# One score matmul per chunk and head in place of seven levels, in a gated linear attention with an FFN

## The chip, the cores and the metric

One core of a Trainium2 chip runs the whole program. TensorE (PE) does the matmuls and the transposes, VectorE (DVE), ScalarE (ACT) and GpSimd (POOL) the elementwise work, SyncE (SP) starts most of the DMAs. Every engine works through its instructions in the order in which the program lists them. The metric is the device time of one execution in microseconds; the profile is of one execution with the hardware profiler on. A matmul on 32-bit floats is two instructions in the trace, each with its own weight load; a transpose is one.

## The reference

```python
f = 1.0 / (1.0 + np.exp(-f_logit))                 # q, k, v, f_logit: (4, 8, 768, 48), float32
for t in range(S):
    state = f[:, :, t, :, None] * state + np.einsum('bhd,bhe->bhde', k[:, :, t], v[:, :, t])
    y[:, :, t] = np.einsum('bhd,bhde->bhe', q[:, :, t], state)
x = y.transpose(0, 2, 1, 3).reshape(B * S, H * D)  # 3072 x 384
g = x @ w_gate                                     # 384 x 1536, float64 as the program gets it
out = (g / (1 + np.exp(-g)) * (x @ w_val)) @ w_out # 1536 x 384, float64
```

In f_logit the values are normal with mean 2 and deviation 0.5.

## The kernel before

The sequence is cut into 6 chunks of 128 tokens; a batch and a chunk are a *unit* (24 of them, in the order of batches, then chunks). Two heads share a transposed tile: head 2a in partitions 0 to 47, head 2a + 1 in partitions 64 to 111, so a unit has 4 head pairs.

`attention(u)` takes a unit in steps that end at a `yield`. The sigmoid of f, then 12 transposes of f, k and q (L147) and their copies out of PSUM. One score matmul per head of q on k gives the diagonal (L169). Then seven levels (m = 1, 2, 4 ... 64, L178 to L202): 8 matmuls of 64 columns (L189), a product on VectorE that puts the next level's gates into q (L192), one on GpSimd for k (L194), one on GpSimd that multiplies neighbouring gates (L197), and a masked copy of the level's scores into A (L198). After that y = state and A on v (L209, L212), the change of the state (kT back by 4 transposes, L221, then 8 matmuls, L225), and the transposes of x (L247). Attention has two PSUM buffers of two banks.

`mlp(g)` is the FFN of 384 tokens (three units): 12 pieces `hidden(j)` with 3 gate and 3 val matmuls of 384 columns (L260), Silu on ScalarE (L263) and the product on VectorE (L265), and 3 pieces `down` of 12 matmuls (L270). PSUM has 3 banks for gate and val and 1 for down.

The order is written out by the loop at the end (L283 to L294): each step of a unit is issued, and after every second step one piece of the list `todo`. That list first holds the 18 pieces in which the weights are fetched (SyncE's queue) and converted from 64-bit floats (768 columns each: seven instructions on VectorE, L116 to L124, and a product on GpSimd, L125), later the FFN pieces of the three units just finished. Unit loads (f, q, k, v, 192 KB each) are issued two units ahead on SyncE's queue, outputs on ScalarE's.

Of the kernel before, what the change touches and what calls it, by code (L numbers as in the profile page):

```python
# [8 lines left out]
FP32 = mybir.dt.float32  # L9
I32 = mybir.dt.int32  # L10
U32 = mybir.dt.uint32
AF = mybir.ActivationFunctionType
ALU = mybir.AluOpType


@with_exitstack
def kernel(
    ctx: ExitStack,
    tc: tile.TileContext,
    q: bass.AP,  # L20
    k: bass.AP,
    v: bass.AP,
    f_logit: bass.AP,
    moe_w_gate: bass.AP,
    moe_w_val: bass.AP,
    moe_w_out: bass.AP,
    out: bass.AP,
):

# [8 lines left out]
    nc = tc.nc  # L40
    B, H, S, D = q.shape
    C = 128
    NCH = S // C
    HP = H // 2
    W = 64
    DM = H * D
    KT = DM // 128
    DFF = moe_w_out.shape[0]
    NF = DFF // 128
    GROUP = 3  # L50
    TB = GROUP * C
    LEVELS = [1, 2, 4, 8, 16, 32, 64]
    NRAW = 3
# [4 lines left out]
    const = ctx.enter_context(tc.tile_pool(name="const", bufs=1))  # L58
    att = ctx.enter_context(tc.tile_pool(name="att", bufs=2))
    ffn = ctx.enter_context(tc.tile_pool(name="ffn", bufs=2))  # L60
    wst = ctx.enter_context(tc.tile_pool(name="wst", bufs=2))
    aps = ctx.enter_context(tc.tile_pool(name="aps", bufs=2, space=bass.MemoryType.PSUM))
    fps = ctx.enter_context(tc.tile_pool(name="fps", bufs=3, space=bass.MemoryType.PSUM))


    ident = const.tile([128, 128], FP32, tag="ident", name="ident")
    make_identity(nc, ident)
    masks = {}
    for m in LEVELS:
# [7 lines left out]
    raw = {nm: [const.tile([128, H, W], FP32, tag=f"{nm}raw{i}", name=f"{nm}raw{i}") for i in range(NRAW)]  # L77
           for nm in "qkf"}
# [4 lines left out]
    w_gate = const.tile([128, KT, DFF], FP32, tag="w_gate", name="w_gate")  # L83
    w_val = const.tile([128, KT, DFF], FP32, tag="w_val", name="w_val")
    w_out = const.tile([128, NF, DM], FP32, tag="w_out", name="w_out")


    units = [(b, c) for b in range(B) for c in range(NCH)]
    vt = {}
# [41 lines left out]
    states = [const.tile([128, HP, 2, D], FP32, tag=f"state{i}", name=f"state{i}") for i in range(3)]  # L131
    for s in states:
        nc.gpsimd.memset(s, 0.0)
    state = {}
    xT = {}
# [158 lines left out]
        todo.pop(0)()  # L294


# [1 line left out]
_INS = ['q', 'k', 'v', 'f_logit', 'moe_w_gate', 'moe_w_val', 'moe_w_out']  # L298
_OUTS = [((3072, 384), 'float32')]
# [27 lines left out]
```

## Time and profile before

| | us |
|---|---|
| median of 3 runs (lowest, highest) | 1121.28 (1120.48, 1121.81) |
| the profiled execution | 1120.95 |
| its span, first to last instruction | 1119.0 |
| TensorE busy in it | 995.0 |
| mean granted clock of TensorE | 0.917 |

The span is what the profile's views cut up; the profiled execution's time has 1.95 us around it. A matmul's end is modelled, and matmuls overlap, so the distance from one start to the next tells more than a busy time.

### The profile page before, as it was taken

The numbers are of one execution on the slowest core, as the hardware profiler recorded it, in microseconds if no ns is written. First come the engines' busy times: TensorE is split into PE (matmuls) and PEld (weight loads), VectorE is DVE, ScalarE is ACT, GpSimd is POOL, SyncE is SP. The second block draws the span as 40 slices with busy tenths as digits, with TensorE's granted clock in tenths as the row PEclk, the third lists the DMA queues.
The fourth block names the chain that finished last, engine by engine and source line by source line (L and its number), as shares of the span: only waits on it lengthen the run. The fifth ranks groups of instructions, "written<-read, shape, count | busy, mean of one in ns | idle before, by whom it ended". The sixth has DMA issues, their size and how long they took to land.

```text
span 1119.0 us, 14668 instructions
## 1 busy us (share of the span) xinstructions
PE 995.0 (89%) x6104; PEld 686.2 (61%) x6104; DVE 434.0 (39%) x660; ACT 166.6 (15%) x288; POOL 281.2 (25%) x419
## 2 busy tenths in 40 slices
PE   3536489998999989998999989998999989998998
PEld 3535466666666566666666576665666666665654
DVE  5999973421432233422333223422333324423010
ACT  1001021120122011220121111220121110110110
POOL 4364541311322121321221221311221222312000
PEclk9955579997999979998899979999899979999899
DMA  9444310010111010110110110110110100000000
GB/s 189 125 138 110 116 29 14 16 36 18 26 29 26 18 36 8 22 36 15 29 29 8 36 36 1 29 36 15 29 29 8 36 8 1 1 1 22 1 1 21
DMA packets 106721, 38.68 MB, mean 35 GB/s; under 512 B 100512, under 2 KB 103584, under 8 KB 106656
## 3 DMA queue, kind: packets, MB, share of 16 engines
q1 hardware_dynamic: 103200, 33.04, 13.6%
q10 hardware_dynamic: 3456, 4.72, 1.2%
q8 instruction: 48, 0.79, 0.3%
q14 instruction: 17, 0.14, 0.0%
HBM read 33.03 MB, written 4.72 MB: 34 GB/s over the span
## 4 chain that ended last, share of the span: by engine, by line
PE 82%; DVE 14%; issue 2%; POOL 1%; ACT 0%; DMA 0%; SPq 0%; DVEq 0%; POOLq 0%; ACTq 0%
PE gate L260 17%; PE val L260 16%; PE o L270 16%; PE sc L189 15%; PE y L212 5%; DVE A L198 4%; DVE qT L192 3%; PE y L209 3%; PE fkT L147 2%; PE sc L169 2%; PE dS L225 1%; DVE man L124 1%; DVE p L116 1%; PE dS L221 1%; PE xTp L247 1%
## 5 line engine op out<-in xcount | busy, mean ns | idle before, releaser
L189 PEld LDWEIGHTS sc<-qT,kT 48*128 48x128 f32 x2688 | 186.8, 210 | 167.7 <-issue 95.1
L189 PE MATMUL sc<-qT,kT 48*128 48x64 f32 x2688 | 210.2, 301 | 89.0 <-DVE A L198 65.5
L260 PE MATMUL gate<-xT,w_gate 128*128 128x384 f32 x576 | 234.9, 518 | 0.6 <-ACT xT L249 0.6
L194 POOL TENSOR_TENSOR kT<-kT,e 128x256 f32<-128x256 f32 x144 | 121.2, 842 | 400.6 <-PE sc L189 400.6
L260 PE MATMUL val<-xT,w_val 128*128 128x384 f32 x576 | 201.9, 486 | 0.0
L270 PE MATMUL o<-w_out,h 128*128 128x384 f32 x576 | 197.0, 493 | 1.1 <-ACT ob L273 1.1
L260 PEld LDWEIGHTS val<-xT,w_val 128*128 128x128 f32 x576 | 109.6, 190 | 76.5 <-issue 0.6
L265 DVE TENSOR_TENSOR h<-silu,val 128x384 f32<-128x384 f32 x96 | 53.2, 555 | 249.9 <-PE val L260 248.2
L270 PEld LDWEIGHTS o<-w_out,h 128*128 128x128 f32 x576 | 105.8, 190 | 69.8 <-ACT ob L273 2.4
L198 DVE COPY_PREDICATED A<-mask,sc 128x512 f32<-128x512 int32 x168 | 146.6, 873 | 0.0
L192 DVE TENSOR_TENSOR qT<-qT,e 128x256 f32<-128x256 f32 x144 | 62.9, 436 | 215.1 <-PE sc L189 215.1
L260 PEld LDWEIGHTS gate<-xT,w_gate 128*128 128x128 f32 x576 | 96.9, 193 | 40.0 <-issue 2.3
L263 ACT ACTIVATE silu<-gate 128x384 f32<-128x384 f32 x96 | 47.1, 490 | 330.5 <-PE gate L260 330.3
L197 POOL TENSOR_TENSOR e<-fT 128x256 f32<-128x256 f32 x24 | 15.6, 652 | 253.5 <-ACT fT L154 253.5
L212 PE MATMUL y<-v,A 128*128 128x48 f32 x384 | 70.4, 323 | 2.7 <-issue 2.7
L212 PEld LDWEIGHTS y<-v,A 128*128 128x128 f32 x384 | 67.7, 249 | 8.1 <-issue 4.0
L215 ACT COPY x<-y 128x384 f32<-128x384 f32 x24 | 11.5, 478 | 282.7 <-PE y L212 282.7
L209 PE MATMUL y<-state,qT 128*128 128x96 f32 x160 | 43.9, 366 | 8.0 <-DVE qT L192 8.0
L192 DVE TENSOR_TENSOR qT<-qT,fT 128x256 f32<-128x256 f32 x24 | 26.0, 1084 | 53.5 <-PE sc L189 53.5
L197 POOL TENSOR_TENSOR e<-e 128x128 f32<-128x128 f32 (+1 forms) x144 | 41.6, 289 | 9.6
L273 ACT COPY ob<-o 128x384 f32<-128x384 f32 x24 | 11.5, 478 | 216.8 <-PE o L270 216.8
L173 DVE TENSOR_TENSOR A<-sc,ident 128x1024 f32<-128x1024 f32 x24 | 29.4, 1223 | 35.7 <-PE sc L169 35.7
(51 smaller groups left out, 617.4 us busy)
## 6 DMA issues: line engine op xcount, KB each, us to landing
fraw<-in_f_logit_dram SPq DMA_DIRECT2D x24, 192.0 KB, 3.0
qraw<-in_q_dram SPq DMA_DIRECT2D x24, 192.0 KB, 3.7
kraw<-in_k_dram SPq DMA_DIRECT2D x24, 192.0 KB, 4.2
v<-in_v_dram SPq DMA_DIRECT2D x24, 192.0 KB, 2.6
w<-in_moe_w_gate_dram SPq DMA_DIRECT2D x6, 768.0 KB, 5.3
w<-in_moe_w_val_dram SPq DMA_DIRECT2D x6, 768.0 KB, 4.2
w<-in_moe_w_out_dram SPq DMA_DIRECT2D x6, 768.0 KB, 4.3
out_dram<-ob ACTq DMA_DIRECT2D x24, 192.0 KB, 1.9
```

What stands on the lines that cost most here:

```text
L173: nc.vector.tensor_tensor(A, sc.rearrange("p r (a t) -> p (r a) t", t=C), ident.unsqueeze(1).broadcast_to((128, H, C)), ALU.mult)
L189: nc.tensor.matmul(sc[:, par, o + 64 * a:o + 64 * a + 64].rearrange("p (n r) -> p n r", r=m), lhsT=kT[r, a, :], rhs=qv[r, a, :, 1, :], sta ...
L192: nc.vector.tensor_tensor(qv[:, :, :, 1, :], qv[:, :, :, 1, :], ev[:, :, :, 0:1].broadcast_to((128, HP, n, m)), ALU.mult)
L194: nc.gpsimd.tensor_tensor(kv[:, :, :, 0, :], kv[:, :, :, 0, :], ev[:, :, :, 1:2].broadcast_to((128, HP, n, m)), ALU.mult)
L197: nc.gpsimd.tensor_tensor(E, ev[:, :, :, 0], ev[:, :, :, 1], ALU.mult)
L198: nc.vector.copy_predicated(A.rearrange("p g (n two r) -> p g n two r", two=2, r=m)[:, :, :, 1, :], masks[m].rearrange("p (n r) -> p n r", ...
L209: nc.tensor.matmul(both, lhsT=qT[:, a, :], rhs=state[b, c - 1][:, a, :, :].rearrange("p r d -> p (r d)"), start=True, stop=False, skip_gro ...
L212: nc.tensor.matmul(both[:, par * D:(par + 1) * D], lhsT=A[:, par * HP + a, :], rhs=vt[u][:, 2 * a + par, :], start=(c == 0), stop=True, sk ...
L260: nc.tensor.matmul(dst, lhsT=w[:, i, j * 128:(j + 1) * 128], rhs=xT[g][:, i, :], start=(i == 0), stop=(i == KT - 1))
L263: nc.scalar.activation(sg, gp, AF.Silu)
L265: nc.vector.tensor_tensor(h[j], sg, vp, ALU.mult)
L270: nc.tensor.matmul(op, lhsT=h[j][:, s * C:(s + 1) * C], rhs=w_out[:, j, :], start=(j == 0), stop=(j == NF - 1))
```

## The change

The program before becomes `general_path`, unchanged. A new `short_path` runs first and computes the whole output. In it a unit's gates are transposed before the sigmoid, with a column of zeros ahead of each head pair, and two scans on VectorE run along them: `tail`, backwards, is the product of all gates from a token to the chunk's end, `head`, forwards, is the product from the chunk's start, divided by the whole chunk's product. k times the tail and q times the head then need one matmul per head for all scores, and a causal mask on VectorE in two passes. The smallest whole product seen is kept in `least`; at the end it is compared with 2^-60, and only if it is below, `general_path` runs too and writes the output again.

Units are ordered by chunks, then batches. The FFN works on one chunk of all four batches (512 tokens). `take_turns` spreads the 20 attention steps of chunk c + 1 over the 28 FFN pieces of chunk c (gate and val are pieces of their own); chunk 0's attention comes first, alone. Weights are fetched and converted in other pieces (256 columns of all three row blocks), with five instructions on VectorE, two on ScalarE and two on GpSimd. Loads run three units ahead. All PSUM buffers are single banks, 4 for attention, 4 for the FFN.

```diff
+    units = [(b, c) for c in range(NCH) for b in range(B)]
...
+            kept["w"] = wst.tile(shape[:2] + [2 * shape[2]], I32, tag="w64", name="w64", bufs=3)
+            nc.sync.dma_start(out=kept["w"], in_=src)
...
+            nc.vector.tensor_single_scalar(top, hi, (1 << 20) - 1, op=ALU.bitwise_and)
+            nc.scalar.activation(man, top, AF.Identity, bias=1.0, scale=2.0 ** -20)
+            nc.scalar.activation(sign, hi, AF.Sign)
+            nc.vector.tensor_scalar(p2, hi, 20, 0x7FF, op0=ALU.logical_shift_right, op1=ALU.bitwise_and)
+            nc.vector.tensor_scalar(p2, p2, 1023 - 127, 1023 + 128, op0=ALU.max, op1=ALU.min)
+            nc.vector.tensor_scalar(p2, p2, 1023 - 127, 1 << 23, op0=ALU.subtract, op1=ALU.mult)
+            nc.gpsimd.tensor_tensor(sign, sign, p2.bitcast(FP32), ALU.mult)
+            nc.vector.scalar_tensor_tensor(man, lo.bitcast(U32), 2.0 ** -52, man, op0=ALU.mult, op1=ALU.add)
+            nc.gpsimd.tensor_tensor(dst, man, sign, ALU.mult)
...
+        p = transposed("fTp", fr)
+        nc.scalar.activation(pairs(gate)[:, :, 1:N1], p, AF.Sigmoid)
+        yield
+        nc.vector.tensor_tensor_scan(tail[:, 0:n][:, ::-1], gate[:, 0:n][:, ::-1], ones[:, ::-1], 1.0,
+                                     op0=ALU.mult, op1=ALU.add)
+        whole = pairs(tail)[:, :, 1:2]
+        kp = transposed("kTp", kr)
+        nc.vector.tensor_tensor(kT, kp, pairs(tail, 2)[:, :, 0:C], ALU.mult)
+        nc.vector.tensor_tensor(least, least, whole.rearrange("p a t -> p (a t)"), ALU.min)
+        nc.vector.tensor_single_scalar(pairs(start)[:, :, 0:1], whole, LEAST, op=ALU.max)
+        nc.vector.reciprocal(pairs(start)[:, :, 0:1], pairs(start)[:, :, 0:1])
+        nc.vector.tensor_tensor_scan(head, gate[:, 0:n], start, 1.0, op0=ALU.mult, op1=ALU.add)
+        qp = transposed("qTp", qr)
+        nc.vector.tensor_tensor(qT, qp, pairs(head)[:, :, 1:N1], ALU.mult)
+        if u + NRAW < len(units):
+            load(u + NRAW)
+        if c:
+            nc.gpsimd.tensor_tensor(decayed, states[b], whole.unsqueeze(2).broadcast_to((128, HP, 2, D)), ALU.mult)
+        yield
...
+                nc.tensor.matmul(sc[par][:, a * C:(a + 1) * C], lhsT=kT[r, a, :], rhs=qT[r, a, :], start=True, stop=True)
+        for par in range(2):
+            nc.vector.tensor_tensor(A[:, par], sc[par].rearrange("p (a t) -> p a t", t=C),
+                                    causal.unsqueeze(1).broadcast_to((128, HP, C)), ALU.mult)
...
+        order = sorted((2 * b + s, b) for b in range(B) for s in range(n_steps))
...
+    for i, f in enumerate(attention_steps(0)):
+        f()
+        if i in (2, 4, 6):
+            fetches.pop(0)()
+        if i in (10, 13, 16, 19):
+            weights()
+    for c in range(NCH):
+        pieces = mlp(c)
+        if c == 0:
+            hidden, pieces = pieces[:2 * NF], pieces[2 * NF:]
+            hidden = [f for i in range(0, 2 * NF, 2) for f in hidden[i:i + 2] + [weights]]
+            pieces = hidden + [weights] * (len(converts) - NF) + pieces
+        take_turns(pieces, attention_steps(c + 1) if c + 1 < NCH else [])
...
+    short_path(tc, least, *args)
+    nc.vector.tensor_reduce(low, least, axis=mybir.AxisListType.X, op=ALU.min)
...
+        nc.tensor.transpose(row, low, ident)
+        nc.vector.tensor_reduce(one, row, axis=mybir.AxisListType.X, op=ALU.min)
+    nc.vector.tensor_single_scalar(flag, one, LEAST, op=ALU.is_lt)
+    redo = nc.values_load(flag[0:1, 0:1], min_val=0, max_val=1, skip_runtime_bounds_check_because="a comparison")
+    with tc.If(redo > 0):
+        general_path(tc, *args)
```

## Rows read from the trace of the kernel before

**Rows 1.** The page's busy time, share and instructions of each engine, whole span.

```profile
PE 995.0 (89%) x6104; PEld 686.2 (61%) x6104; DVE 434.0 (39%) x660; ACT 166.6 (15%) x288; POOL 281.2 (25%) x419
```

**Rows 2.** The page's chain that ended last, by engine.

```profile
PE 82%; DVE 14%; issue 2%; POOL 1%; ACT 0%; DMA 0%; SPq 0%; DVEq 0%; POOLq 0%; ACTq 0%
```

**Rows 3.** Busy time by stretch: engines, then PE's granted clock, DMA share, GB/s.

```profile
112.00:140.00 28.00, 12.50 (x103) 11.19 (x100) 27.16 (x33) 0.22 (x1) 14.37 (x12) 0.50 0.34 115
...
400.00:500.00 100.00, 97.82 (x634) 66.75 (x634) 34.05 (x54) 20.72 (x35) 24.55 (x41) 0.96 0.14 27
```

**Rows 4.** Longest pieces of the chain in order of time: start, length, what.

```profile
363.15 6.65 PE o L270 x20
...
999.33 6.65 PE o L270 x20
...
1050.00 1.94 PE val L260 x6
...
1090.64 7.75 PE o L270 x24
```

**Rows 5.** Timeline, steady state: start, length, instruction, count, idle before and releaser.

```profile
537.92 1.16 PE L169 MATMUL sc<-q,kT 48*128 48x128 f32 x16
...
539.01 0.91 PE L260 MATMUL gate<-xT,w_gate 128*128 128x384 f32 x2
...
564.39 1.90 PE L212 MATMUL y<-v,A 128*128 128x48 f32 x16
...
566.13 0.88 PE L260 MATMUL gate<-xT,w_gate 128*128 128x384 f32 x2
...
568.78 0.60 PE L221 MATMUL dS<-ident,kT 128*128 128x128 f32 x4
...
569.22 0.49 PE L247 MATMUL xTp<-ident,x 128*128 128x128 f32 x3
...
570.28 0.67 PE L225 MATMUL dS<-v,kt 128*64 128x48 f32 x16
...
570.88 1.56 PE L260 MATMUL gate<-xT,w_gate 128*128 128x384 f32 x4
```

**Rows 6.** Groups by line and shape: busy us, mean ns, idle before, releasers.

```profile
L189 PE MATMUL sc<-qT,kT 48*128 48x64 f32 x2688 | 210.2, 301 | 89.0 <-DVE A L198 65.5 <-POOL kT L194 11.0 <-DVE qT L192 8.8
...
L192 DVE TENSOR_TENSOR qT<-qT,fT 128x256 f32<-128x256 f32 x24 | 26.0, 1084 | 53.5 <-PE sc L189 53.5
L124 DVE SCALAR_TENSOR_TENSOR man<-w,man 128x768 f32<-128x768 uint32 x18 | 25.8, 1434 | 0.0
...
L116 DVE TENSOR_SCALAR p<-w 128x768 int32<-128x768 int32 x18 | 19.7, 1095 | 0.1
...
L156 DVE COPY kT<-fkT 128x512 f32<-128x512 f32 x24 | 16.6, 691 | 50.0 <-ACT fT L154 49.9
...
L118 DVE TENSOR_SCALAR p<-p 128x768 int32<-128x768 int32 x18 | 13.0, 720 | 0.0
...
L125 POOL TENSOR_TENSOR w_gate<-man,p 128x768 f32<-128x768 f32 x6 | 11.9, 1990 | 6.8 <-DVE p L119 5.9 <-DVE man L124 0.9
...
L121 DVE TENSOR_SCALAR top<-w 128x768 int32<-128x768 int32 x18 | 11.5, 638 | 0.0
...
L117 DVE TENSOR_SCALAR p<-p 128x768 int32<-128x768 int32 x18 | 10.3, 572 | 0.0
```

**Rows 7.** Timeline of VectorE in the opening, a conversion with nothing on GpSimd.

```profile
49.70 0.55 DVE L117 TENSOR_SCALAR p<-p 128x768 int32<-128x768 int32 x1
...
51.11 0.95 DVE L124 SCALAR_TENSOR_TENSOR man<-w,man 128x768 f32<-128x768 uint32 x1
```

**Rows 8.** Timeline: the first unit's first scores, TensorE.

```profile
10.19 2.08 PE L169 MATMUL sc<-q,kT 48*128 48x128 f32 x16 [2.04 <-DVE kT L156]
```

**Rows 9.** Timeline: the end of the program.

```profile
1107.52 8.01 PE L270 MATMUL o<-w_out,h 128*128 128x384 f32 x24 [0.57 <-ACT ob L273]
...
1116.07 0.34 ACTq L275 DMA_DIRECT2D out_dram<-ob  x1
```

More of the change, by code (lines that the diff above doesn't have):

```diff
@@ L13, with general_path @@
 ALU = mybir.AluOpType
+LEAST = 2.0 ** -60
 @with_exitstack
[L17 to L28, printed above, removed]
+def general_path(ctx, tc, q, k, v, f_logit, moe_w_gate, moe_w_val, moe_w_out, out):
     nc = tc.nc
@@ new lines, with kernel @@
+@with_exitstack
+def kernel(
+    ctx: ExitStack,
+    tc: tile.TileContext,
+    q: bass.AP,
+    k: bass.AP,
+    v: bass.AP,
+    f_logit: bass.AP,
+    moe_w_gate: bass.AP,
+    moe_w_val: bass.AP,
+    moe_w_out: bass.AP,
+    out: bass.AP,
+):
+    nc = tc.nc
+    args = (q, k, v, f_logit, moe_w_gate, moe_w_val, moe_w_out, out)
+    HP = q.shape[1] // 2
+    flags = ctx.enter_context(tc.tile_pool(name="flags", bufs=1))
+    least = flags.tile([128, HP], FP32, tag="least", name="least")
+    short_path(tc, least, *args)
+    low = flags.tile([128, 1], FP32, tag="low", name="low")
+    nc.vector.tensor_reduce(low, least, axis=mybir.AxisListType.X, op=ALU.min)
+    with tc.tile_pool(name="flagp", bufs=1, space=bass.MemoryType.PSUM) as pool:
+        ident = flags.tile([128, 128], FP32, tag="idf", name="idf")
+        make_identity(nc, ident)
+        row = pool.tile([1, 128], FP32, tag="row", name="row")
+        nc.tensor.transpose(row, low, ident)
+        one = flags.tile([1, 1], FP32, tag="one", name="one")
+        nc.vector.tensor_reduce(one, row, axis=mybir.AxisListType.X, op=ALU.min)
+    flag = flags.tile([1, 1], I32, tag="flag", name="flag")
+    nc.vector.tensor_single_scalar(flag, one, LEAST, op=ALU.is_lt)
+    redo = nc.values_load(flag[0:1, 0:1], min_val=0, max_val=1, skip_runtime_bounds_check_because="a comparison")
+    with tc.If(redo > 0):
+        general_path(tc, *args)
```

199 lines of the change are left out of this document (added).

## The prediction

> **What bounds the kernel now.** I read the busy shares first [rows 1]: TensorE is busy for 995.0 of 1119.0 us, no other engine half as long. The chain of waits says the same by time [rows 2]: 82% of it is TensorE, 14% VectorE. But the stages differ [rows 3]: at 112 to 140 us TensorE is busy for 12.5 of 28 us at a granted clock of 0.50 (the 1.2 GHz level) while VectorE is busy for 27.16, so the opening is bound by VectorE, which there converts the 64-bit weights; at 400 to 500 us TensorE is busy for 97.8 of 100 us at 0.96. The steady state repeats per group of 384 tokens: the long down products of 363.15 and 999.33 us are five groups apart [rows 4], so a group takes 636.2 / 5 = 127.2 us.
>
> What a group consists of at the 2.4 GHz level: a gate or val product is 1.94 us, a down product 7.75 us [rows 4], so the FFN is 24 x 1.94 + 3 x 7.75 = 69.8 us. For the attention I take starts to next starts on TensorE [rows 5]: 16 score instructions (8 matmuls, each in two passes) 539.01 - 537.92 = 1.09 us, and a level's 16, with as many weight loads, as much; 16 of y 1.74 us, so 0.109 each; four transposes 0.44 us; 16 of dS 0.60 us. A unit (one batch, one chunk of 128 tokens) without its levels: 19 transposes 2.1, scores 1.09, y (24 instructions with the state) 2.6, dS 0.60, together 6.4 us. Seven levels add 7.6 us. Three units are 42.0 us, with the FFN 111.8; the other 15.4 us of the group, 5.1 per unit, are stalls and half-clock stretches. The levels' matmuls show 89.0 us of idle ahead of them, 3.7 per unit, mostly for VectorE's masked copy and the two products of the next level [rows 6].
>
> **The change part by part.**
>
> *The levels go.* Per unit 112 TensorE instructions, seven masked copies, seven products and seven on GpSimd each for k and e. On the path: 7.6 us of matmuls and 3.7 us of waits per unit, 271 us in 24 units.
>
> *What takes their place on VectorE.* Two scans of 516 columns. The trace has no scan. From below, the nearest two-operation instruction does 768 columns in 0.95 us when nothing disturbs it [rows 7], so 0.64; from above, the slowest form per column, 256 in 1.084 us [rows 6], gives 2.2. I take 1.2: the first row doubled, since each element needs the one before it. Four passes of 512 columns over PSUM (k, q, two score masks) at the 0.691 of the PSUM copy [rows 6], two state updates of 192 columns at about half that (an estimate), four tiny ones at 0.2 (an estimate; bounds 0 and 0.69): 2.4 + 2.8 + 0.7 + 0.7 = 6.6 us per unit, 26 per chunk of four units. With 12 val products of 512 columns, 8.3, VectorE has 35 us of work per 125: hidden in steady state. The order gives it room: between the second step of a unit (k and q transposed, scans) and the third (scores) stand two FFN products, 5.2 us, against some 4.4 us of scan, products and scan.
>
> *Blocks of 512.* Gate and val stream 512 columns: 1.94 x 512 / 384 = 2.58 us. A chunk's FFN is 24 x 2.58 + 4 x 7.75 = 92.9 us; six of them cost what eight groups of 69.8 did, so this part alone moves nothing. It sets the order, though: one chunk of all four batches, whose attention (20 steps) is spread over the 28 FFN pieces of the chunk before. The last chunk's FFN stands alone: 92.9 us, against 69.8.
>
> *Steady chunk.* 92.9 + 4 x 6.4 = 118.5. Each of 20 changes between FFN and attention costs about 0.25 (in [rows 5] the two gate passes that begin at 539.01 and their like run 0.1 to 0.2 over their pitch), 5 us; at a chunk's end the last xT copy is exposed, 1.2 us (an estimate: the idle 0.57 ahead of a matmul that waits for a copy [rows 9], and the copy itself). 124.7 us. Chunks 1 to 3: 374. Chunk 4, beside an attention without kt and dS: 120.5.
>
> *Conversion.* VectorE keeps five instructions a piece: 19.7 + 10.3 + 13.0 + 11.5 + 25.8 = 80.3 us over 18 pieces, 4.46 each [rows 6]. Undisturbed they would be four of 0.55 and one of 0.95 [rows 7], 3.15; the rest is waiting beside GpSimd, which did one product of 1.99 us a piece [rows 6] and now does two. ScalarE takes two more; it is 15% busy [rows 1], and 36 instructions even at 0.95 are 34 us over a stage of 150. For VectorE I take 5.5 a piece, between 3.15 (no disturbance) and 4.46 + 1.99 = 6.45 (the second product blocks for its full length), nearer the upper end: 99 us in all.
>
> *Opening.* All four units of chunk 0 come first, at the 1.2 GHz level: the first scores take 2.08 us at 10.19 us [rows 8] against 1.16 warm, so PE terms double. The new first scores start at about the same time. From one unit's scores to the next, in TensorE's order: scores 2.1, f transposes 0.9, kt 0.9, y 3.5, dS 1.2, k and q 1.8, then some 3.6 of scan and products that nothing covers: 14 us. The third unit's q product ends at 38 us, where VectorE meets the first conversion. From there to the last one it has: conversions 99, the rest of units 2 and 3 8.7, the part of chunk 1's attention that is issued before the last piece (17 of 20 steps) 24.3, val products 8.3, in sum 140; at the share of 0.97 that it reached before [rows 3] 145 us, so the last weight is ready at 183 us. TensorE has 92.9 + 25.6 + 5 in that stage from 67 us on, and waits. Behind it: four down products 31, three attention steps 5, the copy 1.2: chunk 0 ends at 220 us.
>
> *Queues.* Bytes are unchanged (the same 96 unit loads and 18 weight loads). On SyncE's queue weight load n + 3 waits for conversion n, and unit loads stand behind it; they are for units three ahead, needed some 40 us later. The DMA share is 0.34 at 112 us [rows 3]. PSUM goes from two pairs and 3 + 1 banks to 4 + 4 single ones; a product's bank must be free three products (7.7 us) later, a Silu and one pass of 0.69 away. I cost both at nothing.
>
> *The end.* The flag: two reductions, a transpose, a compare, a register load on each engine, a jump. From below, nothing (the last output DMA, issued at 1116.07, ends the span 2.9 us later [rows 9] and may cover it); from above two further DMA-like round trips and ten tiny steps, 8. I take 5. The Trainium skill (Runtime: NRT & Kernel Launch, section Instruction fetch mechanics) says that a taken branch whose target isn't in the current pages stalls for a fetch; no run here shows it, and jumping over the whole old program is such a case, so it speaks for more than zero.
>
> Sum: 220 + 374 + 120.5 + 92.9, then 3.5 from the last matmul to the span's end as before [rows 4, 9], and 5: 816. The profiled execution is 1120.95 for a span of 1119.0, so 818; it lies 0.3 us under the median of the runs, which needs no correction.
>
> **The rivals.**
>
> GpSimd holds VectorE for the full length of both its products. Then 6.45 a piece, 17 us more: 835. For it: the 0.95 us instruction has a mean of 1.434 [rows 6, 7]. Against: 4.46 - 3.15 is only 1.3 per product of 1.99. The Trainium skill (SBUF — State Buffer, section Who interferes with whom) has it as an exclusive lock held for the whole instruction, which is this case.
>
> The conversions hide. With 3.15 a piece and scans of 0.64 VectorE needs 95 us from 38 us on, and TensorE is the bound from 67 us: 67 + 124.7 = 192, so 790. Against: the means above.
>
> The stalls stay. If a unit still loses 5.1 us where I give (5 + 1.2) / 4 = 1.6, because scores now wait for a serial chain of two scans, four overlapped attentions lose 4 x 4 x 3.5 = 56: 874. Against: 3.7 of the 5.1 stand ahead of the levels' matmuls, and 1.4 is left.
>
> Slower: the branch is taken, and the whole old program runs behind the new one: 818 + 1119 = 1937. It decides at a chunk's product of gates below 2^-60. The reference's inputs (seed 0) give 2^-30.5 as the smallest of all, and padded rows give 1, so only an error in the flag would do it.
>
> **How the numbers follow.** The forecast (800 to 850) 0.50, lock 0.13, hidden conversions 0.16, stalls 0.18, branch 0.03. So 818, and 770 to 880: the low end is the hidden case with an end of nothing and fewer changes, the high end the stall case. Under 0.2% (2.2 us, about what this measurement tells from no change) no case falls: faster 0.96, same 0.01, slower 0.03.
>
> **What would show it.** In the windows, VectorE over 90% busy and TensorE well below until the last w_out piece, near 183 us; later TensorE over 95% busy at a clock near 1. Down products of one batch about 125 us apart from chunk to chunk. A scan's mean near 1.2 us. Wrong: TensorE idle on scans or masks in the steady chunks by more than 2 us a unit; the first gate product later than 80 us; more than 10 us behind the last matmul; instructions of the old levels in the trace.

## The result, and the profile after

The changed kernel takes 799.63 us (median of 4 runs, 797.71 to 803.19), the kernel before 1121.55 beside it (4 runs, 1120.48 to 1122.26): a ratio of 0.713 (95% interval 0.711 to 0.716), 322 us less. The profiled execution is 797.71 us for a span of 796.0; the forecast of 818 was 18 us above the median and 20 above the profiled execution, well inside its range.

First the page of the kernel after: busy time, share of the span and instructions of each engine, then the chain of waits by engine, which answer to [rows 1, 2].

```profile
PE 739.0 (93%) x3129; PEld 433.5 (54%) x3129; DVE 296.8 (37%) x430; ACT 183.0 (23%) x264; POOL 96.6 (12%) x79
...
PE 82%; DVE 12%; issue 2%; ACT 2%; POOL 2%; DMA 0%; DVEq 0%; POOLq 0%
```

TensorE lost half of its instructions and 256 us of busy time, and is still 82% of the chain: the bound is the same engine with less to do. The windows (stretch, its length, busy time of each engine, granted clock, DMA share, GB/s) show the two stages that [rows 3] showed.

```profile
28.00:56.00 28.00, 12.84 (x78) 11.40 (x79) 24.92 (x34) 7.56 (x11) 12.89 (x6) 0.55 0.53 135
112.00:140.00 28.00, 15.56 (x52) 7.87 (x50) 27.89 (x28) 8.26 (x11) 18.62 (x9) 0.88 0.47 135
220.77:340.81 120.04, 119.96 (x540) 69.98 (x541) 33.94 (x56) 27.66 (x40) 3.33 (x4) 1.00 0.16 34
```

In the opening TensorE still works for about half of the time and VectorE nearly always; in the steady chunk of the last row TensorE is busy for 119.96 of 120.04 us at the full clock and VectorE for 33.94. The chain in order of time (start, length, what) gives the boundaries of the chunks, as [rows 4] did for the groups:

```profile
220.77 2.84 PE gate L539 x6
...
340.81 2.84 PE gate L539 x6
...
460.85 2.84 PE gate L539 x6
...
580.89 2.84 PE gate L539 x6
...
696.45 2.84 PE gate L539 x6
...
758.51 30.96 PE o L555 x96
```

Three chunks of 120.04 us to the hundredth, one of 115.56, and the last FFN alone, 93.0 to the last matmul. With the first gate product and the end of the program, from the timelines of the two kernels (start, length, instruction, idle time before it), the whole gain can be split. Before:

```profile
154.22 1.96 PE L260 MATMUL gate<-xT,w_gate 128*128 128x384 f32 x4
```

After, with the flag's matmul and the last output's DMA:

```profile
69.48 3.90 PE L539 MATMUL gate<-xT,w_gate 128*128 128x512 f32 x6
...
789.31 0.27 PE L630 MATMUL row<-idf,low 128*1 128x128 f32 x1
...
789.93 0.14 DVE L634 TENSOR_SCALAR flag<-one 1x1 int32<-1x1 f32 x1
790.02 0.34 ACTq L560 DMA_DIRECT2D out_dram<-ob  x1
```

| stretch | before | after | difference |
|---|---|---|---|
| start to first gate product | 154.2 | 69.5 | -84.7 |
| from there to the last matmul's end | 961.3 | 720.0 | -241.3 |
| from there to the end of the span | 3.5 | 6.5 | +3.0 |

The FFN itself is 558 us in both (8 x 69.8, 6 x 92.9), so in the middle stretch all that is not FFN fell from 403 us to 163. The 163 are 58.4 in chunk 0 (220.77 - 69.48 - 92.9), three times 27.1, 22.7 and 0.1. A unit beside an FFN costs 27.1 / 4 = 6.8 us where it cost (127.2 - 69.8) / 3 = 19.1 [rows 4]. Chunk 0 is the odd one: 31 us above a steady chunk. What TensorE waited for up to 221 us says most of why (total us, times, longest):

```profile
PE sc L478 <- DVE qT L465: 29.3, 6, 7.1
PE y L498 <- DVE A L480: 9.5, 2, 5.0
PE y L495 <- DVE A L480: 6.9, 1, 6.9
PE fTp L442 <- DMA fraw<-in_f_logit_dram: 3.6, 1, 3.6
PE gate L539 <- ACT h L546: 0.5, 1, 0.5
```

and from 221 us to the end the same view has one line:

```profile
PE gate L539 <- ACT xT L522: 0.6, 1, 0.6
```

So in 575 us TensorE waits once, for 0.6 us. In the opening it waits 45.7 us for the attention's products on VectorE, and besides them only for the very first load and once for a Silu. No weight is in the list. Of the 45.7 us, 25.4 stand ahead of the first gate product and 20.2 behind it, in chunk 0. The other 11 of chunk 0's 31 us fit the lower level of TensorE's clock behind these waits: 16 score instructions take 2.08 us at 125.09 us, right after a wait of 7.1, and 1.16 at 164.09. The timeline of one of these waits, on GpSimd, VectorE and TensorE:

```profile
82.97 1.99 POOL L402 TENSOR_TENSOR sign<-sign,p 128x768 f32<-128x768 f32 x1 [3.09 <-DVE p L401]
...
83.21 2.17 DVE L399 TENSOR_SCALAR p<-w 128x768 int32<-128x768 int32 x1
...
85.04 2.00 POOL L404 TENSOR_TENSOR w_gate<-top,sign 128x768 f32<-128x768 f32 x1
...
85.42 2.04 DVE L400 TENSOR_SCALAR p<-p 128x768 int32<-128x768 int32 x1
...
88.25 0.55 DVE L401 TENSOR_SCALAR p<-p 128x768 int32<-128x768 int32 x1
...
89.32 0.68 DVE L457 TENSOR_TENSOR kT<-kTp,tails 128x512 f32<-128x512 f32 x1
89.92 0.68 DVE L465 TENSOR_TENSOR qT<-qTp,head 128x512 f32<-128x512 f32 x1
...
90.65 2.08 PE L478 MATMUL sc<-qT,kT 48*128 48x128 f32 x16 [6.20 <-DVE qT L465]
```

A conversion instruction that takes 0.55 us with GpSimd idle (88.25) takes 2.17 and 2.04 beside GpSimd's two products, about as long as these run; k's and q's products stand behind such instructions in VectorE's list, and the scores wait 6.2 us for them.

### The profile page after: what moved, and what is told of

The parts are those of the page before. It is cut to its first block, busy times and chain, and to the rows that moved or that the text cites. A ratio compares the mean times of both kernels' runs of the same rounds, so it can differ in the third digit from the quotient of the medians.

```text
span 796.0 us, 7687 instructions
## 1 busy us (share of the span) xinstructions
PE 739.0 (93%) x3129; PEld 433.5 (54%) x3129; DVE 296.8 (37%) x430; ACT 183.0 (23%) x264; POOL 96.6 (12%) x79
## 4 chain that ended last, share of the span: by engine, by line
PE 82%; DVE 12%; issue 2%; ACT 2%; POOL 2%; DMA 0%; DVEq 0%; POOLq 0%
PE o L555 23%; PE gate L539 21%; PE val L539 21%; PE y L498 5%; PE sc L478 3%; DVE p L399 3%; PE y L495 2%; PE dS L505 2%; DVE top L393 2%; DVE head L462 1%; DVE p L400 1%; DVE top L403 1%; PE kt L485 1%; PE fTp L442 1%; PE kTp L442 1%
## 5 line engine op out<-in xcount | busy, mean ns | idle before, releaser
L539 PE MATMUL gate<-xT,w_gate 128*128 128x512 f32 x432 | 201.9, 604 | 1.4 <-ACT xT L522 0.6
L539 PE MATMUL val<-xT,w_val 128*128 128x512 f32 x432 | 199.3, 597 | 0.0
L550 DVE TENSOR_TENSOR h<-h,val 128x512 f32<-128x512 f32 x72 | 49.3, 684 | 189.0 <-PE val L539 188.0
L546 ACT ACTIVATE h<-gate 128x512 f32<-128x512 f32 x72 | 42.8, 596 | 206.7 <-PE gate L539 206.5
L480 DVE TENSOR_TENSOR A<-sc,causal 128x512 f32<-128x512 f32 x48 | 30.9, 685 | 94.9 <-PE sc L478 94.9
L478 PE MATMUL sc<-qT,kT 48*128 48x128 f32 x384 | 32.6, 318 | 29.3 <-DVE qT L465 29.3
L478 PEld LDWEIGHTS sc<-qT,kT 48*128 48x128 f32 x384 | 27.4, 216 | 44.4 <-DVE qT L465 32.2
L402 POOL TENSOR_TENSOR sign<-sign,p 128x768 f32<-128x768 f32 x18 | 38.1, 2115 | 71.3 <-DVE p L401 62.0
L495 PE MATMUL y<-decayed,qT 128*128 128x96 f32 x160 | 33.9, 295 | 6.9 <-DVE A L480 6.9
L462 DVE TENSOR_TENSOR_SCAN head<-gates,starts 128x516 f32<-128x516 f32 x24 | 38.0, 1584 | 0.7
L495 PEld LDWEIGHTS y<-decayed,qT 128*128 128x128 f32 x160 | 26.7, 198 | 15.7 <-issue 14.4
```

The costliest lines, as they stand in the source:

```text
L402: nc.gpsimd.tensor_tensor(sign, sign, p2.bitcast(FP32), ALU.mult)
L462: nc.vector.tensor_tensor_scan(head, gate[:, 0:n], start, 1.0, op0=ALU.mult, op1=ALU.add)
L478: nc.tensor.matmul(sc[par][:, a * C:(a + 1) * C], lhsT=kT[r, a, :], rhs=qT[r, a, :], start=True, stop=True)
L480: nc.vector.tensor_tensor(A[:, par], sc[par].rearrange("p (a t) -> p a t", t=C), causal.unsqueeze(1).broadcast_to((128, HP, C)), ALU.mult)
L495: nc.tensor.matmul(both, lhsT=qT[:, a, :], rhs=decayed[:, a, :, :].rearrange("p r d -> p (r d)"), start=True, stop=False, skip_group_check ...
L539: nc.tensor.matmul(p, lhsT=w[:, i, j * 128:(j + 1) * 128], rhs=xT[c][:, i, :], start=(i == 0), stop=(i == KT - 1))
```

## The experiments

**Each half of the change alone.** e5_scan_only keeps the order of units, the groups of 384 and the conversion of before and puts scans and one score matmul in place of the levels, with an FFN piece after every step, since there are fewer steps. e6_order_only is the kernel after with the seven levels back, 12 steps a unit and one unit after another over the 28 FFN pieces. Neither has the branch. The core of both edits:

```diff
 # e5_scan_only, against the kernel before
-    aps = ctx.enter_context(tc.tile_pool(name="aps", bufs=2, space=bass.MemoryType.PSUM))
+    aps = ctx.enter_context(tc.tile_pool(name="aps", bufs=4, space=bass.MemoryType.PSUM))
...
+        nc.vector.tensor_tensor_scan(tail[:, 0:n][:, ::-1], gate[:, 0:n][:, ::-1], ones[:, ::-1], 1.0,
+                                     op0=ALU.mult, op1=ALU.add)
...
+        nc.vector.tensor_tensor_scan(head, gate[:, 0:n], start, 1.0, op0=ALU.mult, op1=ALU.add)
...
-        for i, m in enumerate(LEVELS):
...
-            if todo and n % 2 == 1:
+            if todo:
                 todo.pop(0)()
 # e6_order_only, against the kernel after
-        nc.vector.tensor_tensor_scan(head, gate[:, 0:n], start, 1.0, op0=ALU.mult, op1=ALU.add)
...
+        for i, m in enumerate(LEVELS):
...
-        n_steps = 5
-        order = sorted((2 * b + s, b) for b in range(B) for s in range(n_steps))
+        n_steps = 12
+        order = [(0, b) for b in range(B) for s in range(n_steps)]
```

> One part alone: the kernel before (its order by batches, its groups of 384 tokens, its seven-instruction conversion) with the two scans and one score matmul per head in place of the levels, and an FFN piece after every attention step. No branch. First theory: the levels' matmuls and the waits ahead of them are nearly all of the gain. A group is 69.8 + 3 x 6.5 + some 1 = 90 us in place of 127.2, seven of them 632, the opening some 140, the last FFN and the end 73 + 2: 847, between 830 and 880. Rival: the new order is what gains (attention spread evenly, FFN pieces of all batches), and the scans' serial chain stalls one unit at a time; then 950 or more.

> The other part alone: the new kernel's order by chunks, blocks of 512, pieces spread evenly and new conversion, with the seven levels (12 steps a unit, units one after another). No branch. First theory: a chunk keeps 92.9 + 4 x 14 = 149 of matmuls and some 4 x 3.7 of waits, 164; chunk 0's end near 300, since VectorE carries the masked copies and the conversions; 300 + 4 x 164 + 93 + 4 = 1053, between 1020 and 1100. Rival: the even spreading hides the levels' waits and more; 900 to 970.

Measured: e5 824.55 us (824.38 to 830.64), ratio 0.738 (0.734 to 0.741), under the 830 to 880 that I expected; e6 1050.80 (1049.81 to 1056.09), ratio 0.939 (0.935 to 0.942). Against the runs of before beside them (1120.91) the scans alone give 296 us and the order, blocks and conversion alone 70; the whole change gives 322, so the parts overlap. Ahead of the first gate product they need each other: it starts at 105.5 us in e5 and at 175.3 in e6, against 154.2 before and 69.5 with both. The chain of e5 has its groups' down products 89.15 us apart (two groups in 178.30):

```profile
274.46 7.74 PE o L266 x24
...
452.76 7.74 PE o L266 x24
```

which is (89.15 - 69.8) / 3 = 6.5 us per unit, no worse than the 6.8 of the full change. In e6 the chunks are 155.03 us apart, (155.03 - 92.9) / 4 = 15.5 us per unit:

```profile
452.88 7.29 PE o L563 x22
...
607.92 7.29 PE o L563 x22
```

against 14.0 us of matmuls with levels, so the new order and blocks by themselves remove 3.6 of the 5.1 us of stalls of each unit (which of the two does it, e6 doesn't separate). With scans there are no such stalls left to remove. What order, blocks and conversion still add to the scans, the 25 us between e5 and the full change, therefore lies outside the steady state: in e5 TensorE waits 60.8 us for q's product in the opening, 36.1 of them at once.

**Is the scan hidden?** e7_scans_twice runs the forward scan three times in chunks 2 to 5.

```diff
+        if c >= 2:
+            nc.vector.tensor_tensor_scan(head, gate[:, 0:n], start, 1.0, op0=ALU.mult, op1=ALU.add)
+            nc.vector.tensor_tensor_scan(head, gate[:, 0:n], start, 1.0, op0=ALU.mult, op1=ALU.add)
```

> The forward scan three times over instead of once in the units of chunks 2 to 5 (16 units, which run beside FFN pieces). First theory: VectorE has 35 us of work in a steady chunk of 120, and the 2 x 1.23 = 2.46 us more per unit hide in the two FFN products between the steps (5.2 us against 4.4 that are needed): a steady chunk stays at 120.0 or gains under 3 us, the time within 8 us of 799.6. Rival: scores wait for the scans in every unit; 16 x 2.46 = 39 us more, about 839.

800.78 us (797.84 to 802.92), beside 799.63 without: no difference that shows, and its steady chunks are 120.04 us again. Beside an FFN the scans cost nothing, and 2.5 us more per unit would cost nothing either.

**What does the conversion cost?** e2_no_conversion fetches the weights as before but copies only two columns of each piece; the weights stay at a constant, which GpSimd fills in at the start. e3_products_on_vector moves both products of a conversion from GpSimd to VectorE. e4_bits puts the 32-bit float together from the words of the 64-bit one in three instructions of VectorE, with the last bit cut off (right for weights in the normal range of 32-bit floats).

```diff
 # e2_no_conversion
+    for t in (w_gate, w_val, w_out):
+        nc.gpsimd.memset(t, 0.01)
...
+            nc.vector.tensor_copy(dst[:, :, 0:2], kept["w"][:, :, 0:2])     # in place of the conversion
 # e3_products_on_vector
-            nc.gpsimd.tensor_tensor(sign, sign, p2.bitcast(FP32), ALU.mult)
+            nc.vector.tensor_tensor(sign, sign, p2.bitcast(FP32), ALU.mult)
-            nc.gpsimd.tensor_tensor(dst, man, sign, ALU.mult)
+            nc.vector.tensor_tensor(dst, man, sign, ALU.mult)
 # e4_bits, in place of the conversion
+            nc.vector.tensor_scalar(top, hi, 3, 0x3FFFFFF8, op0=ALU.logical_shift_left, op1=ALU.bitwise_and)
+            nc.vector.scalar_tensor_tensor(top, hi, -(1 << 30), top, op0=ALU.bitwise_and, op1=ALU.bitwise_or)
+            nc.vector.scalar_tensor_tensor(dst.bitcast(I32), lo, 29, top, op0=ALU.logical_shift_right, op1=ALU.bitwise_or)
```

> The new kernel with the weights fetched but not converted: in place of nine instructions a piece, one copy of two columns that keeps the order of the fetches (the weights are a constant then). First theory: the opening is bound by VectorE, which spends 5.4 us on each of 18 pieces; without them chunk 0 and its FFN run at TensorE's pace, 67 + 120 = 187 or earlier in place of 220.8, so 30 to 40 us go, 760 to 770. Rival: the opening is bound by the four serial attentions at the 1.2 GHz level and by the loads, and conversion only fills VectorE's gaps; then under 10 us go, 790 or more.

> The two products of a conversion on VectorE in place of GpSimd. First theory: while GpSimd multiplies, VectorE's conversion instructions wait for it for nearly as long, so GpSimd saves VectorE nothing: undisturbed the seven instructions are 4 x 0.55 + 3 x 0.95 = 5.05 us, against the 5.40 that five take now, and the time is the same or up to 6 us less, 793 to 800. Rival: the waits fall where VectorE had nothing to do anyway; then 2 x 0.95 us a piece come on top, 34 us of VectorE, and the time goes to 820 to 835.

> A conversion of three instructions on VectorE and none elsewhere: the 32-bit float put together from the 64-bit one's words with shifts and masks (it cuts the last bit instead of rounding, and holds for magnitudes between 2^-126 and 2^128). First theory: 0.55 + 2 x 0.95 = 2.45 us a piece without waiting, 44 us in place of 97, so VectorE no longer bounds the opening: close to the kernel without conversions, 765 to 778. Rival (the opening is bound by the serial attentions and the loads): 790 or more.

| | median (lowest, highest) | ratio (95%) | first gate | chunk 0's end |
|---|---|---|---|---|
| after | 799.63 (797.71, 803.19) | 0.713 (0.711, 0.716) | 69.5 | 220.8 |
| e2, no conversion | 760.04 (757.60, 765.70) | 0.679 (0.675, 0.682) | 62.9 | 183.1 |
| e3, all on VectorE | 763.64 (761.47, 766.24) | 0.681 (0.679, 0.683) | 62.2 | 186.8 |
| e4, three instructions | 756.72 (754.90, 759.31) | 0.675 (0.673, 0.677) | 58.9 | 179.7 |

e4 came in under the 765 to 778 that I expected. By e2 the whole conversion costs the changed kernel 39.6 us: 6.6 ahead of the first gate product and 31.1 in chunk 0, which in e2 is 120.2 us long, a steady chunk. But e2 has a cost of its own, which shows in its chain:

```profile
7.41 8.89 DVE starts L446
...
18.62 2.08 PE sc L465 x16
```

Beside GpSimd's three fills of the weights (3.94 us each) a VectorE instruction of four columns lasts 9 us (0.16 in the kernel after), and the first scores start at 18.62 us in place of 9.85. Without these 8.8 us the conversion would be worth some 48 us (an estimate, 39.6 + 8.8), which would also account for e4, which does convert, being 3 us faster than e2. And e3, which gives VectorE seven instructions a piece in place of five, is 36 us faster; both of my expectations missed that. Its rows by line and shape (busy us, mean ns), its waits and its window:

```profile
L399 DVE TENSOR_SCALAR p<-w 128x768 int32<-128x768 int32 x18 | 9.9, 549 | 0.0
...
L402 DVE TENSOR_TENSOR sign<-sign,p 128x768 f32<-128x768 f32 x18 | 17.2, 956 | 0.0
...
PE sc L478 <- DVE qT L465: 14.4, 5, 4.4
...
112.00:140.00 28.00, 28.00 (x129) 15.62 (x126) 27.80 (x46) 15.00 (x20) 2.74 (x2) 1.00 0.51 143
```

The same two lines in the kernel after, where L402 is GpSimd's:

```profile
L399 DVE TENSOR_SCALAR p<-w 128x768 int32<-128x768 int32 x18 | 26.3, 1471 | 0.0
...
L402 POOL TENSOR_TENSOR sign<-sign,p 128x768 f32<-128x768 f32 x18 | 38.1, 2115 | 71.3 <-DVE p L401 62.0 <-DVE starts L460 7.8 <-ACT h L546 1.5
```

A product takes VectorE 0.956 us that takes GpSimd 2.115, and without GpSimd L399 falls from 1.471 to 0.549. The seven instructions of a piece need 91.4 / 18 = 5.08 us, less than the five did beside GpSimd (97.2 / 18 = 5.40). VectorE stays as full at 112 to 140 us (27.80 of 28), but TensorE now works through all of that stretch at the full clock. e4's three instructions need 2.46 us a piece.

**Is it GpSimd's presence, or only a shorter path?** In e3 GpSimd's products also left the conversion's own chain. e8_idle_products is e3 with two products put back on GpSimd that nobody reads (in place, on the sign's tile).

```diff
+            nc.gpsimd.tensor_tensor(sign, sign, man, ALU.mult)
+            nc.gpsimd.tensor_tensor(sign, sign, man, ALU.mult)
```

> The conversion with both products on VectorE (763.6 us), and beside it two products of the same size on GpSimd whose result nobody uses (they multiply the sign tile in place, so the next piece's sign waits for them). First theory, now: GpSimd's products hold up VectorE's instructions (0.55 to over 2 us each), and these stand ahead of the attention's in its queue, for which TensorE waits; so nearly all of the 36 us between this and the kernel with its products on GpSimd come back, and more since VectorE has more to do: 795 to 830. Rival: VectorE's queue was merely put in a worse order there, GpSimd's running costs nothing by itself: 761 to 772.

811.07 us (808.63 to 813.45): 47 more than e3, though nothing reads what was added. VectorE's own instructions are longer:

```profile
L403 DVE SCALAR_TENSOR_TENSOR top<-w,top 128x768 f32<-128x768 uint32 x18 | 32.6, 1810 | 0.0
...
L399 DVE TENSOR_SCALAR p<-w 128x768 int32<-128x768 int32 x18 | 16.2, 901 | 0.0
```

L403 takes 0.953 in e3 and 1.810 here. Over all seven VectorE pays 123.8 us in place of 91.4, and TensorE waits 31.0 us for q's product (e3: 14.4). But the idle products also hold the sign's tile, and ScalarE, which writes the next piece's sign, waits for them:

```profile
ACT sign L397 <- POOL sign L404: 78.9, 17, 8.7
```

TensorE in turn waits 7.2 us for copies on ScalarE (e3: none), and VectorE 6.4 us for the tile that the idle products read. VectorE's list isn't in quite the same order in the two kernels either. So the stretch of VectorE's instructions beside GpSimd is shown; how much of the 47 us it makes is not.

**The same edit in the kernel before.** e11_before_product_on_vector moves the one product of the old conversion to VectorE.

```diff
-            nc.gpsimd.tensor_tensor(dst[:, i:i + n_a, j:j + n_n], man, p2.bitcast(FP32), ALU.mult)
+            nc.vector.tensor_tensor(dst[:, i:i + n_a, j:j + n_n], man, p2.bitcast(FP32), ALU.mult)
```

> The kernel before with the one product of its conversion on VectorE in place of GpSimd. Theory: GpSimd's product holds up VectorE's queue there too. VectorE's own work per piece goes from 6.08 (with waits) to at most 4.65 + 0.95 = 5.6 and the attention behind it is reached sooner: 10 to 30 us less, 1090 to 1111. Rival: one product a piece hides, and 0.95 us more on VectorE cost 17 us: 1130 to 1140.

1123.43 us (10 runs), ratio 1.002 (1.001 to 1.003): 2 us slower, and my theory fell. VectorE's old seven instructions took 109.5 / 18 = 6.08 us a piece; now eight take 110.1 / 18 = 6.12. With one product the time that VectorE loses beside GpSimd is just what the product costs on VectorE: the seven fell by 1.04 us a piece, and the eighth takes 1.07. So "off GpSimd" is no rule by itself: with two products a piece it paid 36 us, with one nothing, in two kernels that differ in more than this (the levels' products stay on GpSimd in e11).

**The branch.** e1_no_branch leaves out the flag and the `If`; e9_bits_no_branch does so in e4, timed beside a repetition of e4.

```diff
-    low = flags.tile([128, 1], FP32, tag="low", name="low")
...
-    with tc.If(redo > 0):
-        general_path(tc, *args)
```

> The new kernel without the flag and the branch (the two reductions, the transpose, the compare, the register load, the old program behind it). First theory: the flag stands on the path at the end. From the issue of the last output DMA to the span's end the new kernel takes 796.0 - 790.0 = 6.0 us, the one before 2.9; so 3 us go, about 797 for a median of 799.6, and the tail is 2.9 again. Rival: a branch over a whole program also costs elsewhere (its code, its jump), 8 us or more go. Third: it is hidden by the last output DMA, nothing goes.

> The kernel with the three-instruction conversion once more, as the measure for the two that follow on the same chip: 756.7 as before, within 2 us.

> The kernel with the three-instruction conversion, without the flag and the branch. With the flag its trace ends some 6 us after the last output DMA's issue, the kernel before needs 2.9. First theory: 3 us go, 753.7. Rival: nothing measurable goes, since the first run without a branch (800.3 against 799.6) did not show it; within 1.5 us of the kernel with it.

e1: 800.34 us (795.11 to 800.99), no difference to 799.63. In its trace the last output's DMA is issued 2.9 us ahead of the end of the span, as in [rows 9], where the branch makes it 6.0 (790.02 to 796.0), but its chunk 0 ended 5.8 us later, with the same work in it. The chains of the kernel after and of e1 show where that comes from:

```profile
20.23 1.76 PE sc L478 x16
24.41 1.69 PE y L498 x14
```

```profile
23.47 2.08 PE sc L478 x16
28.12 3.15 PE y L498 x14
```

In e1's trace TensorE takes the first two units at the pace of its lower level, in that of the kernel after in part at that of the higher one, and the third unit's scores start at 37.87 us against 32.03; from there the distance stays at 5.8. (The clock column of e1's windows reads 1.00 in this stretch, which the pace contradicts.) What set the level was not tried. So the opening varies by more than the branch costs, and e1's time decides nothing, but the stretch behind it does: from chunk 0's end to the end of the span it is 575.2 us with the branch and 572.1 without. e4_again: 757.38 (754.32 to 759.94); e9: 752.34 (751.87 to 756.79), 5.0 less. The same stretch of their traces is 575.4 and 572.5 us, and the tails are 6.1 and 3.2. So behind chunk 0 the branch costs 3 us, all of it at the end; the other 2 of the 5.0 are within what the opening varies.

**A better version.** What is left in e4 is an opening in which TensorE waits for one unit's scans at a time. e10_bits_overlap lets chunk 0's units start one step apart instead of two, with a third set of gate tiles.

```diff
-    NROT = 2
+    NROT = 3
...
-        order = sorted((2 * b + s, b) for b in range(B) for s in range(n_steps))
+        order = sorted(((2 if c else 1) * b + s, b) for b in range(B) for s in range(n_steps))
```

> The kernel with the three-instruction conversion, and chunk 0's four units overlapped by one more step (order by b + s in place of 2 b + s, three sets of gate and scan tiles). First theory: in the opening TensorE waits for the chain of two scans and products ahead of each unit's scores (3.3 + 1.7 + 4.4 + 1.8 = 11 us in the trace); a unit more in flight hides most of it, the first gate product comes at 52 in place of 59 us, the time is 5 to 8 us less, 749 to 752. Rival: VectorE and the clock's lower level set the opening whatever the order; within 2 us of it.

743.24 us (740.00 to 743.57), ratio 0.662 (0.661 to 0.663), 14 us less than e4_again beside it and the fastest version here. I had expected 5 to 8. The first gate product comes at 44.7 us (e4_again 56.3), and the windows of e4_again and then e10 show more work of TensorE in the same stretch, and a higher granted clock:

```profile
28.00:56.00 28.00, 19.88 (x128) 17.67 (x127) 20.60 (x34) 4.16 (x8) 0.00 (x0) 0.61 0.67 175
```

```profile
28.00:56.00 28.00, 26.32 (x144) 18.11 (x143) 20.66 (x34) 6.64 (x11) 0.83 (x1) 0.76 0.71 185
```

## Why the prediction was right, and where it was not

*The levels go: right.* Seven levels were priced at 7.6 us of matmuls and 3.7 of waits, 11.3 a unit and 271 us in all. In the steady state of e5, which keeps the old order, a unit fell from 19.1 us to 6.5, by 12.7: the 11.3, and nearly all of the other 1.4 us of stalls too. e5 as a whole is 296 us faster.

*The steady chunk: 124.7, measured 120.04.* The sum of its matmuls was 118.5; I added 5 for 20 changes between FFN and attention and 1.2 for the xT copy, and only 1.5 is there. The xT copy is covered: at the chunk's end the next unit's transposes stand between the last x transposes and the first gate product.

```profile
459.74 0.49 PE L521 MATMUL xTp<-ident,x 128*128 128x128 f32 x3
460.06 0.60 PE L442 MATMUL fTp<-ident,fraw 128*128 128x128 f32 x4
460.50 0.27 PE L442 MATMUL kTp<-ident,kraw 128*128 128x128 f32 x1
460.85 2.41 PE L539 MATMUL gate<-xT,w_gate 128*128 128x512 f32 x5
```

The mis-sized term is the 0.25 us per change. It rested on 0.1 to 0.2 us that two passes in [rows 5] run over their pitch, raised for the changes of both kinds; why such a surplus doesn't show in the new chunks was not tried. Over three such chunks, the shorter chunk 4 (115.56 for 120.5) and the end, 14 + 5 + 2 = 21 us, which is the whole distance from 818 to 797.7.

*The scan: 1.2 us, right.* The doubled row is 1.28, and I took 1.2; 516 columns take 1.23 us undisturbed:

```profile
L452 DVE TENSOR_TENSOR_SCAN tails<-gates,ones 128x516 f32<-128x516 f32 x24 | 29.6, 1231 | 78.2 <-ACT gates L447 78.2
L462 DVE TENSOR_TENSOR_SCAN head<-gates,starts 128x516 f32<-128x516 f32 x24 | 38.0, 1584 | 0.7
```

(the head's mean holds disturbed ones of up to 2.83). VectorE's 35 us per steady chunk came as 33.9, and e7 shows the cover that I had named.

*The conversion: 5.5 us of VectorE a piece, measured 5.40.* The five lines sum to 26.3, 21.0, 20.3, 19.7 and 9.9, 97.2 us. The rival with a lock for the full length (6.45) overshot by 1 us a piece as a mean. The rule that went with it (the Trainium skill, SBUF — State Buffer, section Who interferes with whom) is borne out one instruction at a time: in the timeline above, VectorE's 0.55 became 2.17 beside a product of 1.99. It costs less on average because a product doesn't always run beside it: L401, the last of the three on the exponent, keeps a mean of 0.549 us.

*The opening: 220 us, measured 220.77, and not for my reason.* I had the conversion start at 38 us, behind the third unit's q product. I had doubled all of TensorE's terms; here the first two units ran in part at the higher level, and that product ended at 31.97 us (37.8 in e1's trace). And the conversion starts at 23.22, ahead of that unit's scan, because the list that VectorE works through isn't in the order of the kernel's text (the code issues the conversion behind that product). By 38 us two of the 18 pieces were through. The last weight was written at 164 us and not at 183:

```profile
162.15 1.82 POOL L404 TENSOR_TENSOR w_out<-top,sign 128x768 f32<-128x768 f32 x1
```

I had TensorE wait for weights, with 37 us of work left behind the last one. It never waited for one; it waited 45.7 us for q's product and the masked scores, all but the first 5.8 us of it with conversions in VectorE's list, and had 57 us left at 164. The two errors, 19 us sooner and 20 us more behind, cancelled, so the agreement is luck; in e1's trace chunk 0 ends at 226.53. The step that failed is "TensorE waits for the last weight". It would have mattered for any edit: by the length of VectorE's list e3 was worth at most 6 us to me, and it gained 36.

*The end: 8.5 us, measured 6.5.* I gave the branch 5 us; the traces of both pairs with and without it give 3. The rule that a taken branch out of the current pages stalls for a fetch (the Trainium skill, Runtime: NRT & Kernel Launch, section Instruction fetch mechanics) fits a cost above zero; no run separates the fetch from the load of the flag.

*The rivals.* "The conversions hide" (790) lies nearer to the result than the forecast does, by the number, but not by what happened: VectorE was full, and leaving out the conversion brought 40 us. "The stalls stay" is ruled out by the 0.6 us of waits after 221 us. The old program did not run.

## What to carry to other kernels

Where two engines work in the same stage, price a helper's instruction by what it does to the other's list, and above all to the instructions of other work that stand in that list behind it: here the waits of the scores, not the late weights, were the cost. Moving work onto the fuller engine can win, and the same edit can be worth nothing where the traded times are equal (e3 and e11), so measure both in the kernel at hand. Look also at what an experiment itself adds: e2's fills on GpSimd took back some 9 us of what it was to show. And a stage total that comes out right is no proof of its steps: check which wait ended last before building on it.

## What the runs showed of the hardware that I had not expected

- Work on GpSimd that nobody needs can cost much: two products per piece whose output is not used made the kernel 47 us slower (e8 against e3; how much of it by the tiles that they hold is open), with the mean of VectorE's L403 up from 0.95 to 1.81 us. And beside three fills of 3.94 us a VectorE instruction of four columns lasted 9 us in place of 0.16 (e2).
- Changes between FFN and attention cost TensorE next to nothing at the full clock: with 20 attention steps among 28 FFN pieces a chunk of 120.04 us is 1.5 us over the sum of its matmuls.
- Fewer waits in the opening came with a higher clock: with TensorE busy for 19.88 of 28 us the granted clock was 0.61, with 26.32 it was 0.76 (e4_again, e10). Taking out waits of 11.9 - 5.0 = 6.9 us on q's product brought 14 us in the median; how the rest divides between clock and order wasn't separated.
- The same work ended chunk 0 at 220.77 us in one run and at 226.53 in another (after, e1_no_branch), all of it by the level at which TensorE took the first two units (14 instructions of y in 1.69 us or in 3.15), while the steady chunks agreed to 0.01 us. Differences under some 6 us in the opening can't be told from one trace.
